# One V block of head 26 on partitions 0 to 63, in two loads of 32 rows

## The chip, the cores and the metric

The kernel runs on one core of a Trainium2 chip. The metric is the device time of one execution in microseconds; less is better. All data is 32-bit floating point.

## The reference, cut to what matters

One token passes through attention and a small MLP, twice, with the same weights and the same caches both times. There are 32 heads, 8192 cached positions and 128 numbers to a head, so each pass reads 128 MB of K and 128 MB of V (the second pass keeps a little of the first's data).

```python
def _A_ref(x, k_cache, v_cache, wq, wo):
    q = (x @ wq).reshape(B, Sq, H, Dh) ...
    scores = jnp.einsum("bhqd,bhkd->bhqk", q, k_cache) * (Dh ** -0.5)
    p = _softmax(scores, axis=-1)
    o = jnp.einsum("bhqk,bhkd->bhqd", p, v_cache)
    return ... o.reshape(B, Sq, H * Dh) @ wo
def _B_ref(x, w1, w2):
    return relu(x @ w1) @ w2

x = x + _A_ref(_layernorm(x), k_cache, v_cache, wq, wo)
x = x + _B_ref(_layernorm(x), w1, w2)
x = x + _A_ref(_layernorm(x), k_cache, v_cache, wq, wo)
x = x + _B_ref(_layernorm(x), w1, w2)
```

## The kernel before, in words

K and V are streamed from device memory through a ring in on-chip memory, `ring`, 128 partitions by 4808 units of 8 numbers. The host lays the caches out beforehand (`_laid_out`), so that each load is one contiguous piece of `kv`, and every partition gets one contiguous row of it. Row sizes in the listings below are in numbers: a load `128x8192` is 128 rows of 8192 numbers, 4 MB.

A head's K is four pieces and its V four blocks; each of the eight is 1 MB. `UNITS` says which pieces share a load. From head 4 to 23 heads are joined, in loads of 6 or 5 MB; heads 24 to 27 have one 4 MB load for K and one for V; heads 0, 1 and 28 to 31 have smaller loads. `ORDER` lists the units, `HEADS` the order of the heads in each pass: 0 to 31 in the first, 31 down to 24 and then the others in the second. Some units of heads 29 to 31 are kept from the first pass to the second.

What sets the order of the loads is `pump`. It takes the next unit of the list `todo`, asks `place` for room in the ring, issues the load on SP's queue, and goes on until no room is left. `release`, called after the last product that reads a piece, frees its room and calls `pump` again. SP issues in that order and waits, for each load, until the products that read the old data are done, and until an earlier load has landed whose completion semaphore the new load takes over. A few loads of weights are issued by ScalarE (ACT's queue).

For each head TensorE multiplies the K pieces with the query (`scores`), VectorE takes the maximum, ScalarE the exponentials, and `turn` transposes them, one block of 128 columns at a time, in squares of 32 by 32, into `hd.all_p`. `values` then multiplies each V block: four products, one for each strip `g` of 32 output rows, of all 128 partitions with 4 columns of the turned exponentials. A V block lies over all 128 partitions: 128 rows of 2048 numbers. `output` adds up the strips, and the next head begins. After the last head of a pass come the output projection and the MLP, whose loads of weights (`part_of_w2`, `mix`) and whose reuse of the ring join the two passes.

The lines that the prediction's steps touch: the ring loads are L189 in `pump`, the products of `scores` L516, those of `values` L570, the transpositions L552 in `turn`.

Of the kernel before, what the change touches and what calls it, by code (L numbers as in the profile page):

```python
# [10 lines left out]
F32 = mybir.dt.float32  # L11
# [4 lines left out]
P = 128  # L16
D = 640
H = 32
SK = 8192
DH = 128  # L20
# [15 lines left out]
K_ALL = [(r, 0, RUN) for r in range(4)]  # L36
V_ALL = [(b, 0, 4) for b in range(NBL)]
# [3 lines left out]
UNITS = {h: WHOLE for h in range(H)}  # L41
# [12 lines left out]
    ("v", V_ALL[2:]),  # L54
]
UNITS[30] = HALVES
UNITS[28] = [("k", K_ALL[:1]), ("k", K_ALL[1:2])] + HALVES[1:]
UNITS[31] = HALVES[:2] + LAST
PAIR = [
# [10 lines left out]
UNITS = {  # L70
    h: [[(h, kind, piece) for piece in pieces] for kind, pieces in units]
    for h, units in UNITS.items()
}
# [8 lines left out]
ORDER = [(h, i) for h in range(H) for i in range(len(UNITS[h]))]  # L82
# [14 lines left out]

def wide(kind, piece):

    return 4 * piece[2] * (1 if kind == "k" else DH) // 8  # L100


def size(u):
    return sum(wide(kind, piece) for _, kind, piece in UNITS[u[0]][u[1]])
# [17 lines left out]
def w2_width(blocks):  # L122
    return sum(D // 2 if b == FB - 1 else D for b in blocks)
# [3 lines left out]
def decode_kernel(ctx: ExitStack, tc: tile.TileContext, x, kv, wq, wo, wqo, w1, w2, out):  # L127
    nc = tc.nc
    consts = ctx.enter_context(tc.tile_pool(name="consts", bufs=1))
    wts = ctx.enter_context(tc.tile_pool(name="wts", bufs=1))  # L130
    work = ctx.enter_context(tc.tile_pool(name="work", bufs=1))
# [9 lines left out]
    ring = consts.tile([P, 8 * (RING + W2_UNITS)], F32, name="ring")  # L141
# [6 lines left out]

    beside = todo[n_first : n_first + BESIDE]
    del todo[n_first : n_first + BESIDE]  # L150
    dram_at, o = {}, 0
    for u in ORDER:
        dram_at[u] = o
        o += 8 * P * size(u)
    live = {}
    lent = set()
    at_of = {}
# [2 lines left out]
    def place(layer, u, n):  # L160


        step = 8 if u in KEPT else max(m for m in (8, 64, 256, 512) if n % m == 0)
        low, high = 0, FLAT if u[0] >= 28 else 3 * BIG
        if layer and (u[0] >= 28 or u[0] < HG):
            high = RING
        if n > FLAT // 3:
            step, high = BIG, 3 * BIG
        if layer == 0 and u in kept and (u in KEPT or u[0] == 30 and UNITS[30][u[1]][0][1] == "k"):
            low, high = (EDGE, RING) if u in KEPT else (FLAT, EDGE)  # L170
        at, best = low, None
        for a, m in sorted(live.values()) + [(high, 0)]:
            a = min(a, high)
            if a - at >= n and (best is None or a - at < best[1]):
                best = at, a - at
            at = max(at, -(-(a + m) // step) * step)
        return None if best is None else best[0]

    def pump():
        while todo:  # L180
            layer, u = todo[0]
            n = size(u)
            at = place(layer, u, n)
            if at is None:
                return
            todo.pop(0)
            o = dram_at[u]
            stays = PARK_ROW if (layer, u) == (1, PARKED) else 0
            nc.sync.dma_start(  # L189
                ring[:, 8 * at + stays : 8 * (at + n)],  # L190
                kv[o : o + 8 * P * n].rearrange("(p m) -> p m", p=P)[:, stays:],
            )
            if stays:
                for a, bank in parked:
                    nc.scalar.copy(ring[:, 8 * at + a : 8 * at + a + bank.shape[1]], bank)
            for t, (_, kind, piece) in enumerate(UNITS[u[0]][u[1]]):
                m = wide(kind, piece)
                live[layer, u, t] = at, m
                at_of[layer, u, t] = ring, 8 * at
                at += m  # L200
            if not todo or layer < todo[0][0]:
                assert all(a + m <= RING for a, m in live.values())
                live["w2"] = RING, W2_UNITS
                for part in W2_LOADS[layer][:2]:
                    part_of_w2(layer, part, by_parts[:, part[0] * D :])
                if layer == 0:
                    part_of_w2(0, W2_LOADS[0][2], wct.rearrange("p c d -> p (c d)"))
        rest = W2_LOADS[1][2:]
        if (1, rest[0][0]) not in w2_block:
            n = w2_width(sum(rest, ()))  # L210
            at = place(1, (0, None), n // 8)
            if at is not None:
                at *= 8
                for part in rest:
                    part_of_w2(1, part, ring[:, at:])
                    at += w2_width(part)

    def part_of_w2(L, blocks, where):
        loads = W2_LOADS[L]
        o = P * w2_width(sum(loads[: loads.index(blocks)], ()))  # L220
        n = w2_width(blocks)
        nc.sync.dma_start(where[:, :n], w2[L, o : o + P * n].rearrange("(p m) -> p m", p=P))
        at = 0
        for b in blocks:
            m = w2_width((b,))
            w2_block[L, b] = where[:, at : at + m]
            at += m
# [17 lines left out]
    def key(L, u, t):  # L245
        return (0 if u in kept else L), u, t
# [45 lines left out]
    load_wq(0, nc.sync)  # L292
    nc.scalar.dma_start(xr, x)
    pump()
    load_wo(0, 0, nc.sync)

# [251 lines left out]

    def turn(hd):

        for b in range(NBL):
            nc.vector.transpose(hd.all_p[:, b * P : (b + 1) * P], hd.p[:, b * P : (b + 1) * P])  # L552

# [6 lines left out]
        nc.vector.reciprocal(hd.rl, pt[:, :1])  # L560

    def values(hd, piece, where, first, last):
        b, r, m = piece
        tile_of, at = at_of[key(*where)]
        ranges = ((r, r + m),) if hd.out is hd.out_2 else ((r, min(r + m, 2)), (max(r, 2), r + m))
        for r0, r1 in ranges:
            for g in range(4) if r0 < r1 else ():
                i = 4 * b + g
                v = at + (g * m + r0 - r) * DH
                nc.tensor.matmul(  # L570
                    (hd.out if r0 < 2 else hd.out_2)[
                        32 * g : 32 * g + 4, r0:r1
                    ].rearrange("p r d -> p (r d)"),
                    hd.all_p[:, 32 * i : 32 * i + 4],
                    tile_of[:, v : v + (r1 - r0) * DH],
                    start=first,
                    stop=last or (hd.out is not hd.out_2 and b == NBL - 1),
                    skip_group_check=True,
                )
        release(*where)  # L580
# [485 lines left out]
def _laid_out(A_x, A_k_cache, A_v_cache, A_wq, A_wo, B_w1, B_w2):  # L1066
    k = np.asarray(A_k_cache)[0].reshape(H, 4, 4, RUN, DH).transpose(0, 4, 1, 2, 3)
    v = np.asarray(A_v_cache)[0].reshape(H, 4, 4, NBL, 4, 32, DH).transpose(0, 1, 5, 3, 4, 2, 6)
    v = v.reshape(H, P, NBL, 4, 4, DH)
    kv = np.empty(H * P * SK * 2, k.dtype)  # L1070
    o = 0
    for u in ORDER:
        n = 8 * size(u)
        block = kv[o : o + P * n].reshape(P, n)
        o += P * n
        a = 0
        for h, kind, piece in UNITS[u[0]][u[1]]:
            if kind == "k":
                r, c, m = piece
                part = k[h, :, :, r, c : c + m]  # L1080
            else:
                b, r, m = piece
                part = v[h, :, b, :, r : r + m]
            part = part.reshape(P, -1)
            block[:, a : a + part.shape[1]] = part
            a += part.shape[1]
    w2 = np.zeros((P, FB, D), np.asarray(B_w2).dtype)
    for b, f in enumerate(_hidden_rows()):
        w2[f >= 0, b] = np.asarray(B_w2)[f[f >= 0]][:, _COLS]
    w2[W2_LAST:, -1, : D // 2] = w2[:W2_LAST, -1, D // 2 :]  # L1090
    wq = np.asarray(A_wq).reshape(NB, P, NG, HG * DH).transpose(2, 1, 0, 3).reshape(NG, P, HG * D)
    wo = np.asarray(A_wo)[:, _COLS].reshape(NG, HG, DH, D).transpose(0, 2, 1, 3)
    wqo = [
        [np.concatenate([wq[b], wo[a].reshape(P, HG * D)], 1) for a, b in zip(gs[1:-1], gs[2:])]
        for gs in GROUPS
    ]
    return {
        "x": np.repeat(np.asarray(A_x).reshape(D)[_COLS].reshape(4, DR), 32, axis=0),
        "kv": kv,
        "wq": wq.reshape(NG * P, HG * D),  # L1100
        "wo": wo,
        "wqo": np.array(wqo),
        "w1": np.asarray(B_w1).reshape(NB, P, DFF).transpose(1, 0, 2),
        "w2": np.array(
            [
                np.concatenate(
                    [
                        np.concatenate([w2[:, b, : w2_width((b,))] for b in part], 1).reshape(-1)
                        for part in loads
                    ]  # L1110
                )
                for loads in W2_LOADS
            ]
        ),
    }
# [24 lines left out]
```

## Time and profile before

| what | value |
|---|---|
| median of three runs | 1344.15 us (1343.68 to 1344.17) |
| span of the profiled execution, first to last instruction | 1340.6 us |
| TensorE (PE) busy | 874.0 us, 65% |
| VectorE (DVE) busy | 290.2 us, 22% |
| ScalarE (ACT) busy | 62.6 us, 5% |
| moved by DMA | 571.70 MB, 426 GB/s on average |
| mean granted TensorE clock | 0.820 |

The profiled execution is one of its own; its own time is known by its span, 1340.6 us, and the runs' times hold what lies around a span too. A page of the profile has the busy time of each engine, the span in 40 slices, the DMA queues, the chain of work that ended last (followed back from the last instruction to whatever released it), the costliest groups of instructions, and the DMA issues with their size and the time from issue to landing. Other views give the same for a stretch of time. PE is TensorE's products, PEld its weight loads, SP the engine that only issues loads. A product of 32-bit numbers stands as two records on PE. "<-" behind an idle time names what ended it.

### The profile page before, as it was taken

What the parts mean: (1) busy time and instruction counts of PE and PEld (TensorE: products, weight loads), DVE (VectorE), ACT (ScalarE), POOL (GpSimd) and SP (SyncE); (2) the same over time, 40 slices, a digit from 0 to 9 for tenths busy, and PEclk for the clock granted to TensorE, in tenths of its full rate; (3) what the DMA queues carried; (4) which work ended last, traced back from release to release, by engine and by line L of the source; (5) the groups of instructions that cost most, each with busy time, mean ns of one, the idle gap of its engine ahead of it and who ended that gap; (6) DMA issues with size and microseconds to landing.
All of it is one profiled execution on the core that took longest, in us unless ns stands there. A gap on an engine that the chain in (4) does not pass through costs nothing.

```text
span 1340.6 us, 13403 instructions
## 1 busy us (share of the span) xinstructions
PE 874.0 (65%) x5806; PEld 255.5 (19%) x5806; DVE 290.2 (22%) x956; ACT 62.6 (5%) x155; POOL 2.9 (0%) x10
## 2 busy tenths in 40 slices
PE   5463575767657656676688755657566666567687
PEld 2110121111111111112243211112111111111123
DVE  2120121211212112223123212221221212212222
ACT  0000000000000000000000000000000000000000
POOL 0000000000000000000000000000000000000000
PEclk8686787988777887788799977887778787888789
DMA  9999999999999999999999999999999999999998
GB/s 395 431 435 430 442 423 437 429 428 437 432 434 429 428 439 426 433 425 415 425 396 425 430 435 433 432 433 431 433 429 434 432 428 433 437 427 436 425 424 333
DMA packets 24546, 571.70 MB, mean 426 GB/s; under 512 B 2724, under 2 KB 2984, under 8 KB 6952
## 3 DMA queue, kind: packets, MB, share of 16 engines
q1 hardware_dynamic: 21464, 529.31, 92.1%
q10 hardware_dynamic: 3024, 41.53, 7.3%
q8 instruction: 46, 0.75, 0.2%
q14 instruction: 12, 0.10, 0.0%
HBM read 570.83 MB, written 0.00 MB: 426 GB/s over the span
## 4 chain that ended last, share of the span: by engine, by line
DMA 67%; PE 27%; DVE 4%; ACT 1%; issue 1%; SPq 0%; ACTq 0%; DVEq 0%
DMA ring<-in_kv 66%; PE ps L516 10%; PE outs L570 9%; PE side L672 1%; DMA ring<-in_w 1%; DVE p L591 1%; PE acc L621 1%; PE side L440 1%; ACT p L545 1%; DVE h_t L531 1%; PE small L536 1%; PE small L604 1%; PE side L454 1%; DVE p L552 0%; DVE h_t L537 0%
## 5 line engine op out<-in xcount | busy, mean ns | idle before, releaser
L516 PE MATMUL ps<-ring,spread_q 128*32 128x512 f32 (+3 forms) x2088 | 332.7, 727 | 149.2 <-DMA ring<-in_kv 148.6
L570 PE MATMUL outs<-ring,p 128*4 128x512 f32 (+3 forms) x2080 | 310.6, 732 | 164.1 <-DMA ring<-in_kv 95.7
L531 DVE TENSOR_REDUCE h_t<-ps 128x1 f32<-128x512 f32 x64 | 44.3, 691 | 365.4 <-PE ps L516 365.4
L570 PEld LDWEIGHTS outs<-ring,p 128*4 128x4 f32 x2080 | 50.6, 95 | 348.4 <-issue 233.8
L516 PEld LDWEIGHTS ps<-ring,spread_q 128*32 128x32 f32 x2088 | 63.9, 124 | 277.5 <-issue 188.8
L545 ACT ACTIVATE p<-ps,h_t 128x512 f32<-128x512 f32 x63 | 43.3, 687 | 1161.2 <-DVE h_t L537 1161.2
L552 DVE STREAM_TRANSPOSE p<-p 128x128 f32<-128x128 f32 x256 | 79.8, 312 | 63.9 <-ACT p L545 57.2
L587 DVE TENSOR_SCALAR p<-outs,ind 128x128 f32<-128x128 f32 x64 | 22.5, 351 | 317.2 <-PE outs L570 317.2
L604 PE MATMUL small<-ones,p 128*128 128x1 f32 (+1 forms) x128 | 25.3, 267 | 97.4 <-DVE p L591 97.4
L591 DVE SCALAR_TENSOR_TENSOR p<-outs,ind,p 128x128 f32<-128x128 f32 x188 | 66.0, 351 | 6.7
L536 PE MATMUL small<-ident,h_t 128*128 128x128 f32 x128 | 32.7, 339 | 40.1 <-DVE h_t L531 39.9
L604 PEld LDWEIGHTS small<-ones,p 128*128 128x128 f32 x128 | 19.9, 195 | 159.7 <-DVE p L591 158.9
L672 PE MATMUL side<-w_t,wct 128*128 128x448 f32 (+1 forms) x80 | 45.3, 651 | 0.0
L452 DVE TENSOR_SCALAR q_row<-side,ln_r 128x128 f32<-128x128 f32 x56 | 19.5, 349 | 106.0 <-PE ps L516 59.0
L440 PE MATMUL side<-both_t,ln_xc 128*32 128x512 f32 x140 | 37.3, 844 | 0.0
L536 PEld LDWEIGHTS small<-ident,h_t 128*128 128x128 f32 x128 | 20.0, 196 | 89.0 <-DVE h_t L531 85.5
L621 PE MATMUL acc<-both_t,o_cols 128*64 128x320 f32 x220 | 34.6, 458 | 0.0
L454 PEld LDWEIGHTS side<-sel,q_row 128*128 128x128 f32 x112 | 19.3, 216 | 56.3 <-DVE q_row L452 29.9
L537 DVE TENSOR_REDUCE h_t<-small 128x1 f32<-128x128 f32 x64 | 18.7, 292 | 35.4 <-PE small L536 35.4
L454 PE MATMUL side<-sel,q_row 128*128 128x1 f32 x112 | 24.1, 284 | 0.3 <-DVE q_row L452 0.2
L621 PEld LDWEIGHTS acc<-both_t,o_cols 128*64 128x64 f32 x220 | 15.5, 147 | 29.4 <-issue 17.7
L672 PEld LDWEIGHTS side<-w_t,wct 128*128 128x128 f32 x80 | 13.5, 211 | 32.4 <-issue 32.4
(148 smaller groups left out, 219.5 us busy)
## 6 DMA issues: line engine op xcount, KB each, us to landing
ring<-in_kv SPq DMA_DIRECT2D x50, 6144.0 KB, 35.0
ring<-in_kv SPq DMA_DIRECT2D x23, 4096.0 KB, 33.2
ring<-in_kv SPq DMA_DIRECT2D x29, 2048.0 KB, 27.7
both_t<-in_wqo ACTq DMA_DIRECT2D x12, 2560.0 KB, 24.7
ring<-in_kv SPq DMA_DIRECT2D x4, 5120.0 KB, 34.6
ring<-in_kv SPq DMA_DIRECT2D x9, 1024.0 KB, 23.9
w_t<-in_w ACTq DMA_DIRECT2D x1, 4320.0 KB
ring<-in_kv SPq DMA_DIRECT2D x5, 768.0 KB, 29.5
```

The costliest lines, as they stand in the source:

```text
L440: nc.tensor.matmul(pq[32 * strip : 32 * strip + 32], xc[:, c : c + 1].to_broadcast([P, 32]), wq_t[:, c], start=c < 4, stop=c in (1, 2, 3, ...
L454: nc.tensor.matmul(mine[:, :1], row, one_of_each, start=True, stop=True, skip_group_check=True)
L516: nc.tensor.matmul(hd.ps[32 * g : 32 * g + 32, c : c + n], spread_q[:, 3 - r : 35 - r], tile_of[:, at + g * n : at + (g + 1) * n], start=f ...
L531: nc.vector.tensor_reduce(hd.nm, hd.ps, AX.X, ALU.max, negate=True)
L536: nc.tensor.matmul(pt[:, :P], hd.nm.to_broadcast([P, P]), ident, start=True, stop=True)
L545: nc.scalar.activation(hd.p, hd.ps, AF.Exp, bias=hd.low, scale=scale, accum_out=hd.l)
L552: nc.vector.transpose(hd.all_p[:, b * P : (b + 1) * P], hd.p[:, b * P : (b + 1) * P])
L570: nc.tensor.matmul((hd.out if r0 < 2 else hd.out_2)[32 * g : 32 * g + 4, r0:r1].rearrange("p r d -> p (r d)"), hd.all_p[:, 32 * i : 32 * i ...
L591: nc.vector.scalar_tensor_tensor(oc, hd.out[:, r], ind[:, r : r + 1], oc, op0=ALU.mult, op1=ALU.add)
L604: nc.tensor.matmul(pt[:, :n], part, mask.to_broadcast([P, n]), start=i == 0, stop=i == len(parts) - 1,)
L621: nc.tensor.matmul(acc[64 * g : 64 * g + 64, : 2 * DR], col.to_broadcast([P, 64]), wt[:, 2 * DR * g : 2 * DR * (g + 1)], start=first, stop ...
L672: nc.tensor.matmul(pt[:, :n], wct[:, c], w1_t[:, c, f : f + n], start=(c == 0), stop=(c == NB - 1),)
```

## The change

The first V block of head 26 (block 0, 1 MB) gets a unit of its own, `LOW_BLOCK`, and is laid on partitions 0 to 63 only, with rows twice as long: 64 rows of 4096 numbers. Row r holds what partitions r and r + 64 held. In device memory it stands as two times eight groups; a group is four rows, one behind another, and 64 unused numbers follow it, so that neighbouring groups don't run on into each other. `pump` loads it with two loads of 32 rows, each from eight groups. The other three blocks of that V stay one load of 3 MB.

In `turn`, the exponentials of the upper 64 partitions are transposed a second time, into partitions 0 to 63 of a small tile (`by_act`), and `values` multiplies the block in eight products of 64 partitions, four with the lower half and four with that tile. In the ring the block takes twice its former columns (512 units in place of 256): `place` puts it at columns 4096 to 4607 of the units in both passes, above the rest, and the places of some loads after it move. Head 26 is loaded in both passes, so all this happens twice.

```diff
+LOW_BLOCK = (0, 0, 4, "low")
+UNITS[26] = [("k", K_ALL), ("v", [LOW_BLOCK]), ("v", V_ALL[1:])]
...
-    return 4 * piece[2] * (1 if kind == "k" else DH) // 8
+    return 4 * piece[2] * (1 if kind == "k" else DH) // 8 * (1 + is_low(piece))
+def is_low(piece):
+    return len(piece) > 3
+LOW_ENGINES = 8
+LOW_GAP = 64
+def low_group(n):
+    return 32 // LOW_ENGINES * 8 * n + LOW_GAP
...
+            if low_unit(u):
+                m = LOW_ENGINES * low_group(n)
+                for half in range(2):
+                    nc.sync.dma_start(
+                        ring[32 * half : 32 * half + 32, 8 * at : 8 * (at + n)],
+                        kv[o + half * m : o + half * m + m]
+                        .rearrange("(g m) -> g m", g=LOW_ENGINES)[:, : low_group(n) - LOW_GAP]
+                        .rearrange("g (r m) -> g r m", m=8 * n),
+                    )
+            else:
...
     def turn(hd):
+        low = [piece for piece, _ in pieces_of(0, hd.h, "v") if is_low(piece)]
+        for b, *_ in low:
+            hd.upper = work.tile([P, 2, DH], F32, name="by_act")[:64, 0]
+            nc.vector.transpose(hd.upper, hd.p[64:, b * P : (b + 1) * P])
         for b in range(NBL):
             nc.vector.transpose(hd.all_p[:, b * P : (b + 1) * P], hd.p[:, b * P : (b + 1) * P])
...
     def values(hd, piece, where, first, last):
+        if is_low(piece):
+            for half, turned in enumerate((hd.all_p[:64, b * P : (b + 1) * P], hd.upper)):
+                for g in range(4):
+                    v = at + (4 * half + g) * 4 * DH
+                    nc.tensor.matmul(
+                        hd.out[32 * g : 32 * g + 4].rearrange("p r d -> p (r d)"),
+                        turned[:, 32 * g : 32 * g + 4],
+                        tile_of[:64, v : v + 4 * DH],
+                        start=first and half == 0,
+                        stop=last and half == 1,
+                        skip_group_check=True,
+                    )
+            release(*where)
+            return
```

On SP's queue, in the first pass, around heads 24 to 28 (`128x8192` rows are K or V of a whole head), there stands before:

```order
L189 DMA ring<-in_kv 128x12288 x17
L189 DMA ring<-in_kv 128x8192 x8
L189 DMA ring<-in_kv 128x2048 x2
L189 DMA ring<-in_kv 128x4096 x3
L189 DMA ring<-in_kv 128x704
```

and now:

```order
L223 DMA ring<-in_kv 128x12288 x17
L223 DMA ring<-in_kv 128x8192 x5
L216 DMA ring<-in_kv 32x1x4096 x2
L223 DMA ring<-in_kv 128x6144
L223 DMA ring<-in_kv 128x8192 x2
L223 DMA ring<-in_kv 128x2048 x2
```

The load of V of head 26, the sixth of the eight, has become three: two of 32 rows of 4096 numbers and one of 128 rows of 6144. The order of the others is the same; the second pass has the same three in place of one.

On TensorE, at head 26 in the first pass (the rows `side` and `both_t` are the queries of the next group of heads, `small<-ident` the maximum of all rows), before:

```order
L516 MATMUL ps<-ring,spread_q 32x512 x4
L454 MATMUL side<-sel,q_row 128x1
L536 MATMUL small<-ident,h_t 128x128
L570 MATMUL outs<-ring,p 4x512 x4
L454 MATMUL side<-sel,q_row 128x1
L570 MATMUL outs<-ring,p 4x512 x12
L604 MATMUL small<-ones,p 128x1
```

and now:

```order
L550 MATMUL ps<-ring,spread_q 32x512 x4
L488 MATMUL side<-sel,q_row 128x1
L570 MATMUL small<-ident,h_t 128x128
L607 MATMUL outs<-ring,p 4x512 x4
L607 MATMUL outs<-ring,by_act 4x512 x4
L488 MATMUL side<-sel,q_row 128x1
L622 MATMUL outs<-ring,p 4x512 x12
L656 MATMUL small<-ones,p 128x1
```

The first block's four products have become eight, four of them with the second transposition; the other twelve follow as before. On VectorE one transposition of 64 by 128 stands ahead of the head's four.

More of the change, by code (lines that the diff above doesn't have):

```diff
@@ L98, in wide, with low_unit, placed_in_dram @@
 def wide(kind, piece):
-    return 4 * piece[2] * (1 if kind == "k" else DH) // 8
+    return 4 * piece[2] * (1 if kind == "k" else DH) // 8 * (1 + is_low(piece))
+def is_low(piece):
+    return len(piece) > 3
+def low_unit(u):
+    return any(is_low(piece) for _, _, piece in UNITS[u[0]][u[1]])
+LOW_ENGINES = 8
+LOW_GAP = 64
+def low_group(n):
+    return 32 // LOW_ENGINES * 8 * n + LOW_GAP
+def placed_in_dram():
+    at, o = {}, 0
+    for u in ORDER:
+        at[u] = o
+        o += 2 * LOW_ENGINES * low_group(size(u)) if low_unit(u) else 8 * P * size(u)
+    return at, o
 def size(u):
@@ L150, in decode_kernel @@
     del todo[n_first : n_first + BESIDE]
[L151 to L154, printed above, removed]
+    dram_at, _ = placed_in_dram()
     live = {}
@@ L188, in pump @@
             stays = PARK_ROW if (layer, u) == (1, PARKED) else 0
[L189 to L192, printed above, removed]
+            if low_unit(u):
[8 more added lines that the diff above has]
+            else:
+                nc.sync.dma_start(
+                    ring[:, 8 * at + stays : 8 * (at + n)],
+                    kv[o : o + 8 * P * n].rearrange("(p m) -> p m", p=P)[:, stays:],
+                )
             if stays:
@@ L562, in values @@
     def values(hd, piece, where, first, last):
-        b, r, m = piece
+        b, r, m = piece[:3]
         tile_of, at = at_of[key(*where)]
+        if is_low(piece):
[9 more added lines that the diff above has]
+                        skip_group_check=True,
+                    )
+            release(*where)
+            return
         ranges = ((r, r + m),) if hd.out is hd.out_2 else ((r, min(r + m, 2)), (max(r, 2), r + m))
@@ L1069, in _laid_out @@
     v = v.reshape(H, P, NBL, 4, 4, DH)
-    kv = np.empty(H * P * SK * 2, k.dtype)
-    o = 0
+    dram_at, total = placed_in_dram()
+    kv = np.zeros(total, k.dtype)
     for u in ORDER:
-        n = 8 * size(u)
+        n, o = 8 * size(u), dram_at[u]
+        if low_unit(u):
+            ((h, _, (b, *_)),) = UNITS[u[0]][u[1]]
+            block = v[h, :, b].reshape(2, 2, 32, n // 2).transpose(1, 2, 0, 3)
+            m = LOW_ENGINES * low_group(size(u))
+            kv[o : o + 2 * m].reshape(2 * LOW_ENGINES, -1)[:, :-LOW_GAP] = block.reshape(
+                2 * LOW_ENGINES, -1
+            )
+            continue
         block = kv[o : o + P * n].reshape(P, n)
-        o += P * n
         a = 0
```

## The prediction

> **What bounds the kernel now.** I read the page of the profile first: its head, the slices, the queues and the chain of waits.
>
> ```profile
> span 1340.6 us, 13403 instructions
> PE 874.0 (65%) x5806; PEld 255.5 (19%) x5806; DVE 290.2 (22%) x956; ACT 62.6 (5%) x155; POOL 2.9 (0%) x10
> ...
> DMA  9999999999999999999999999999999999999998
> ...
> DMA packets 24546, 571.70 MB, mean 426 GB/s; under 512 B 2724, under 2 KB 2984, under 8 KB 6952
> ...
> q1 hardware_dynamic: 21464, 529.31, 92.1%
> q10 hardware_dynamic: 3024, 41.53, 7.3%
> q8 instruction: 46, 0.75, 0.2%
> ...
> DMA 67%; PE 27%; DVE 4%; ACT 1%; issue 1%; SPq 0%; ACTq 0%; DVEq 0%
> ```
>
> The 16 DMA engines are at work in every slice. The loads of the two hardware queues fill 92.1% + 7.3% = 99.4% of 16 engines' span, while TensorE is busy for 65% of it. So the kernel is a stream of 571.70 MB, and the only room left is in how evenly the 16 engines share it. I therefore looked at short stretches: in the middle of each pass, where the V of head 26 is loaded, and at the two ends of the stream. The columns are the stretch, its length, the busy time of PE, PEld, DVE, ACT and POOL, the granted clock, the busy share of the 16 DMA engines, and GB/s.
>
> ```profile
> 570.00:580.00 10.00, 6.16 (x42) 1.49 (x35) 1.56 (x5) 0.00 (x0) 0.00 (x0) 0.84 1.00 429
> 785.00:795.00 10.00, 5.33 (x34) 1.19 (x34) 2.15 (x8) 0.00 (x0) 0.00 (x0) 0.83 1.00 429
> ...
> 1331.00:1332.00 1.00, 0.74 (x21) 0.63 (x25) 0.17 (x1) 0.00 (x0) 0.00 (x0) 1.00 0.83 334
> 1332.00:1333.00 1.00, 1.00 (x36) 0.96 (x32) 0.00 (x0) 0.00 (x0) 0.00 (x0) 1.00 0.58 242
> 1333.00:1334.00 1.00, 1.00 (x30) 0.71 (x20) 0.08 (x2) 0.00 (x0) 0.00 (x0) 1.00 0.59 242
> 1334.00:1335.00 1.00, 0.99 (x26) 0.76 (x25) 0.87 (x6) 0.00 (x0) 0.00 (x0) 1.00 0.49 197
> 1335.00:1336.00 1.00, 0.81 (x19) 0.59 (x15) 0.23 (x3) 0.00 (x0) 0.15 (x1) 1.00 0.37 133
> 1336.00:1337.00 1.00, 0.96 (x28) 0.39 (x20) 0.00 (x0) 0.00 (x0) 0.40 (x1) 1.00 0.02 8
> ```
>
> In the middle the share is 1.00 and all 16 together move 429 GB/s, so one engine moves 429/16 = 26.8 GB/s. At the end the share falls in steps. From 1332 to 1334 it is 0.58 to 0.59, which is 9 of 16 engines; from 1334 to 1335 it is 0.49 (8), from 1335 to 1336 0.37 (6), and at 1336.4 or so all are done. So seven engines finish the last loads by about 1332.3 and nine need until 1334.3 to 1336.4. The same picture stands at the end of the first pass, just before the load of `mix` is issued (at 692.67 in the chain below) and reaches the idle engines:
>
> ```profile
> 691.50:692.00 0.50, 0.35 (x4) 0.16 (x8) 0.10 (x1) 0.00 (x0) 0.00 (x0) 1.00 1.02 415
> 692.00:692.50 0.50, 0.50 (x12) 0.24 (x8) 0.00 (x0) 0.00 (x0) 0.00 (x0) 1.00 0.71 292
> 692.50:693.00 0.50, 0.50 (x14) 0.25 (x5) 0.32 (x1) 0.00 (x0) 0.00 (x0) 1.00 0.66 248
> 693.00:693.50 0.50, 0.50 (x5) 0.44 (x4) 0.34 (x3) 0.31 (x2) 0.00 (x0) 1.00 0.44 179
> 695.00:695.50 0.50, 0.50 (x24) 0.48 (x20) 0.00 (x0) 0.00 (x0) 0.00 (x0) 1.00 1.06 435
> ```
>
> Some engines are out of work from 692 on (0.71, then 0.66 of 16), only seven still run at 693.25 (0.44), and by 695 all work on what came next. The engines thus drift apart by 3 to 4 us in each pass, although every load gives each of them the same bytes. The 46 packets of the instruction queue are the one thing on the page that can fall on some engines and not on others; the page doesn't say on which. The chain of waits says what the late ones cost:
>
> ```profile
> 573.46 34.55 DMA ring<-in_kv
> 608.14 5.36 PE outs L570 x32
> ...
> 692.67 4.72 DMA mix<-in_w
> 697.43 0.75 PE side L482 x16
> ...
> 1286.31 30.14 DMA ring<-in_kv
> 1316.50 19.15 DMA ring<-in_w
> ```
>
> A load counts as landed when its last engine has delivered. The chain runs through such landings, and its last link ends at 1316.50 + 19.15 = 1335.65, among the nine late engines. The latest engine sets the time; one that is done early saves nothing.
>
> **The change part by part.** *The bytes.* The block is 64 rows of 4096 numbers, 1,048,576 bytes, as before. Before, all 16 engines carry it, 65,536 bytes each, inside the 4 MB load. Now two loads of 32 rows come from eight contiguous groups. No row of this trace shows how such a load is shared out, so its price lies between two bounds: if all 16 engines share it, nothing moves (0); if each group is one engine's, eight engines carry 131,072 bytes each and the other eight none. Then eight gain 65,536 / 26.8 GB/s = 2.45 us of work in each pass and eight lose as much. I take the second, since eight sources of one piece each are nearest to the rows of one engine in the loads there are; both ends stay in the range.
>
> The Trainium skill, "DMA: Bandwidth & Descriptors", under "Why a DMA increments its semaphore by 16 and not by 1", says that a load runs on the largest number of engines up to 16 that divides the slowest dimension of both sides, and on the lowest-numbered ones; 8 and 32 would give eight engines, the same eight twice. No run so far shows it. The same page's "Rules for kernel authors" says of transfers to partition halves that both spray over all 16 engines, so that nothing is won; by that rule the sum would be 0 instead of 2.45 us a pass, which is the first rival below.
>
> *What 2.45 us do at the end of a pass.* Only seven engines have that much slack at the end (those done by 1332.3). Eight get the extra work, so at least one late engine is among them. At best it is the first of the nine, and 1334.3 + 2.45 = 1336.75, or 0.35 us after today's 1336.4; at worst it is the last, +2.45. Six engines end between 1335 and 1336.4. If lateness has nothing to do with the half that is loaded, three of those six are loaded, the last of the three ends about 0.3 us before the last of the six, and the pass gets 2.45 - 0.3 = 2.15 us longer. At the end of the first pass nine engines are idle at 693.25, so the bounds there are 0 and +2.45; the same reasoning gives 2.15. I take 2.15 twice: the rows show no order by halves, and with half of the engines loaded at random the six latest are spared almost never.
>
> *Why it isn't absorbed in between.* Where the stream is full the share is 1.00: the late engines have no idle time that could take the extra work. Between the passes the loads that follow the `mix` load are issued after work that itself waited for the last landing, so a later landing shifts them too.
>
> *Issues on SP.* Each pass has two more loads, three issues instead of one. The rows that show SP's lead are these (size, then median us from issue to landing; then whom SP waits for):
>
> ```profile
> ring<-in_kv SPq DMA_DIRECT2D x23, 4096.0 KB, 33.2
> ring<-in_kv SPq DMA_DIRECT2D x9, 1024.0 KB, 23.9
> ...
> SPq L189 <- DMA ring<-in_kv: 367.3, 77, 20.6
> ```
>
> A 4 MB load takes 4,194,304 / 429 = 9.8 us on the engines and lands 33.2 us after its issue, so SP runs more than 20 us ahead. What hides two more issues, or a load that waits for a later landing, is this lead: 0. If it were gone, a wait of SP on a ring load is 367.3/77 = 4.8 us, once or twice a pass. The block's place at the top of the ring moves the places of the loads around it, and with them what a load waits for: in the first pass the last part of head 28 now waits for two K pieces of head 27 instead of the last V piece of head 26, and in the second pass K of head 27 waits for a V piece of head 29. Both are within the lead.
>
> *TensorE and VectorE.* The block needs eight products of 64 rows in place of four of 128, and one more transposition:
>
> ```profile
> 588.68 1.84 PE L570 MATMUL outs<-ring,p 128*4 128x512 f32 x8 [1.87 <-DMA ring<-in_kv]
> 787.44 4.95 PE L570 MATMUL outs<-ring,p 128*4 128x512 f32 x32 [4.41 <-DMA ring<-in_kv]
> L552 DVE STREAM_TRANSPOSE p<-p 128x128 f32<-128x128 f32 x256 | 79.8, 312 | 63.9 <-ACT p L545 57.2
> ```
>
> These are the first products of head 26's V in the two passes (eight records are four products). They take up to 1.84 us a block, so four more cost up to 1.84 us a pass, and the transposition at most 312 ns, as for a whole block. TensorE waited 1.87 and 4.41 us for the V there. The low block is issued ahead of the other three blocks, so its products fall into that wait: 0. If the cover were gone, the ring would be freed about 2 us later, still within SP's lead.
>
> **Sum:** 2 x 2.15 = +4.3 us on the profiled execution's 1340.6 us span. The median of the runs, 1344.15, lies 3.55 us above that span, which I take to be what lies around it, unchanged: 1344.15 + 4.3 = 1348.4 us.
>
> **The rivals.** *Nothing moves.* The two loads are spread over all 16 engines, as by the rule named above, or the end isn't as tight as the tail says. For it: no row shows a load on eight engines. Against it: the source lies in eight separate pieces. It gives 1344.2 us, with the small costs above within 0.5 us.
>
> *The slack is on the loaded side.* If the seven early engines are all among the eight loaded, the extra falls where there is room. It gives 0.35 us at the end and 0 to 2 us after the first pass, so +0.4 to +2.7: 1346 us. For it: lateness comes in a group (seven against nine), and a group may well follow the engines' numbers. Against it: nothing on the page ties it to a half, and nine don't fit into eight.
>
> *The other side: faster.* The late engines all lie in the lightened half and the loaded half takes its extra inside its slack. Then each pass ends 2.45 us earlier, 2 x 2.45 = 4.9 us: 1339.3 us. It decides from the point where at least eight engines are done 2.45 us before the last. At 692.5 to 693.5 that could be so (9 of 16 idle at the end of it); at 1333 to 1334 the share of 0.59 says nine still run, one too many. Elsewhere the runs without a profile may differ from this one.
>
> **How the numbers follow.** A change of 0.2%, 2.7 us, is about what a measurement of this kernel can tell from none. Extra work on late engines (+3.5 to +4.9, 1347.6 to 1349.1): 0.60. Slack on the loaded side (+0.4 to +2.7, 1344.5 to 1346.9): 0.20. Nothing moves: 0.13. Faster: 0.07. I predict the first, 1348.4. The range must leave out no more than 0.2: it reaches from 1344.3, which takes in the second case and half of the third, to 1349.6, the bound of 2 x 2.45 with the small costs on top. Slower by over 0.2% has the first case and a third of the second: 0.66; within 0.2% the rest of the second and the third: 0.27; faster 0.07.
>
> **What would show it.** If the two loads run on eight engines, the DMA share in the stretch after they start stays at 1.00 but the ends of the passes change: the steps of the tail come at other heights, with some engines done 2.45 us sooner and the last one 2 us later. The chain should keep its links, with the last landing of each pass later by 2.15 us. A new wait of SP or TensorE near 590 or 790 us would show my cover wrong. A tail in which all 16 engines end within a microsecond would be the faster rival; an unchanged tail the first. The prediction is wrong if a load of 32 rows uses all 16 engines, or if lateness follows the halves.

## The result, and the profile after

The changed kernel takes 1348.06 us (median of five, 1346.8 to 1352.15). The kernel before, run beside it, takes 1344.03 (1343.33 to 1344.17). The ratio is 1.0035, with a 95% interval of 1.0023 to 1.0047: 3.1 to 6.3 us slower. The prediction was 1348.4.

The page of the profiled execution, in the order in which that of before was shown:

```profile
span 1345.0 us, 13440 instructions
PE 897.7 (67%) x5822; PEld 259.7 (19%) x5822; DVE 290.9 (22%) x958; ACT 62.5 (5%) x155; POOL 2.9 (0%) x10
...
DMA packets 24706, 571.70 MB, mean 425 GB/s; under 512 B 2756, under 2 KB 3016, under 8 KB 6984
...
q1 hardware_dynamic: 21624, 529.31, 91.9%
...
q8 instruction: 46, 0.75, 0.2%
```

The bytes are the same, and the stream still fills the span (91.9% of 16 engines in q1). The packets say on how many engines the new loads ran. q1 has 160 more than before, and 32 more are under 512 B. e5 below, whose two added loads are plain ones of 128 rows, has 288 packets more than before, 32 of them small: 128 + 16 for each load. So a load shows one data packet for each row and, it seems, one small packet for each engine that carries it. The two passes have four new loads of 32 rows: 4 x 32 = 128 data packets more (the old block's rows were part of longer ones, and that load still has its 128), and 4 x 8 = 32 small ones. By this count each load ran on eight engines. The Trainium skill, "DMA: Bandwidth & Descriptors", under "Why a DMA increments its semaphore by 16 and not by 1", gives eight for sides of 8 and 32; the 32 small packets agree. The other rule that the prediction named, by which both parts would spray over all 16, doesn't hold for these loads.

The stretches of time, columns as in the prediction (busy PE, PEld, DVE, ACT, POOL; granted clock; busy share of 16 DMA engines; GB/s). First the two in the middle of the passes:

```profile
570.00:580.00 10.00, 5.93 (x42) 1.58 (x35) 1.56 (x5) 0.00 (x0) 0.00 (x0) 0.84 0.99 423
785.00:795.00 10.00, 7.22 (x42) 1.27 (x38) 2.59 (x8) 0.78 (x2) 0.00 (x0) 0.67 1.02 440
```

The new loads lie there, and the stream runs on at its old rate. Then the end of the kernel:

```profile
1335.00:1336.00 1.00, 1.00 (x8) 0.94 (x8) 0.62 (x4) 0.37 (x2) 0.00 (x0) 1.00 0.78 315
1336.00:1337.00 1.00, 0.74 (x22) 0.63 (x25) 0.17 (x1) 0.00 (x0) 0.00 (x0) 1.00 0.73 284
1337.00:1338.00 1.00, 1.00 (x36) 0.96 (x32) 0.00 (x0) 0.00 (x0) 0.00 (x0) 1.00 0.33 131
1338.00:1339.00 1.00, 1.00 (x30) 0.71 (x22) 0.07 (x1) 0.00 (x0) 0.00 (x0) 1.00 0.18 74
1339.00:1340.00 1.00, 1.00 (x26) 0.77 (x25) 0.87 (x6) 0.00 (x0) 0.00 (x0) 1.00 0.27 92
1340.00:1341.00 1.00, 0.99 (x22) 0.77 (x22) 0.24 (x3) 0.00 (x0) 0.14 (x1) 1.00 0.07 24
```

and the end of the first pass:

```profile
693.00:693.50 0.50, 0.21 (x2) 0.07 (x1) 0.22 (x1) 0.00 (x0) 0.00 (x0) 1.00 0.35 143
693.50:694.00 0.50, 0.48 (x8) 0.25 (x12) 0.00 (x0) 0.00 (x0) 0.00 (x0) 1.00 0.24 97
694.00:694.50 0.50, 0.50 (x16) 0.20 (x8) 0.00 (x0) 0.00 (x0) 0.00 (x0) 1.00 0.15 61
694.50:695.00 0.50, 0.50 (x10) 0.30 (x2) 0.45 (x2) 0.00 (x0) 0.00 (x0) 1.00 0.22 92
```

Before, nine of 16 engines were late together (0.58, 0.59). Now most are done by about 1337, and some three (0.18) to four (0.27) work alone until after 1340. The first pass ends the same way: 0.15 to 0.24 from 693.5 on. This is what extra work on a few engines that were late already would look like; the trace doesn't say which engines they are. The chain of waits has the first pass's delay in two links:

```profile
650.93 35.21 DMA ring<-in_kv
694.54 5.21 DMA mix<-in_w
```

The first ends at 686.14 (before 648.54 + 35.72 = 684.26), 1.88 us later; `mix` lands at 699.75 (before 697.39), 2.36 us later.

At the end of the kernel the chain doesn't keep its links. Before, its last link was a load, to 1335.65. Now it has no load behind the one that these products wait for (in the kernel before, the same products began at 1289.15 and waited for no load):

```profile
1291.72 1.89 PE L622 MATMUL outs<-ring,p 128*4 128x512 f32 x8 [4.53 <-DMA ring<-in_kv]
```

From 1310 on TensorE waits for a load only once:

```profile
PEld side L987 <- DMA ring<-in_w: 0.3, 1, 0.3
```

So in this execution the lonely engines and TensorE arrive together, and the tail alone doesn't set the end.

How late the stream is can be counted from the packets of the traces: the time at which the two hardware queues have moved a number of MB, less the time before (us; one profiled execution each; e5 and e10 are explained below).

| moved | 270 MB | 310 MB | 320 MB | 570 MB | 570.8 MB |
|---|---|---|---|---|---|
| time before | 630.2 | 727.8 | 751.6 | 1332.1 | 1335.6 |
| changed kernel | +0.1 | +2.4 | +3.2 | +3.3 | +4.2 |
| e5: even shares in both passes | +0.2 | +1.0 | +3.0 | +3.1 | +3.5 |
| e10: eight engines in the first pass only | +0.2 | +1.9 | +2.3 | +2.6 | +2.7 |

Nothing is lost while the block is loaded (270 MB lie behind the first pass's block), nor between 320 and 570 MB. The changed kernel loses 2.3 us up to 310 MB, around the end of the first pass, 0.8 us behind it, where e5 loses more, and 0.9 us in the last 0.8 MB.

### The profile page after: what moved, and what is told of

The parts are those of the page before. It is cut to its first block, busy times and chain, and to the rows that moved or that the text cites. A ratio compares the mean times of both kernels' runs of the same rounds, so it can differ in the third digit from the quotient of the medians.

```text
span 1345.0 us, 13440 instructions
## 1 busy us (share of the span) xinstructions
PE 897.7 (67%) x5822; PEld 259.7 (19%) x5822; DVE 290.9 (22%) x958; ACT 62.5 (5%) x155; POOL 2.9 (0%) x10
## 3 DMA queue, kind: packets, MB, share of 16 engines
q1 hardware_dynamic: 21624, 529.31, 91.9%
## 4 chain that ended last, share of the span: by engine, by line
DMA 60%; PE 32%; DVE 5%; ACT 1%; issue 1%; SPq 0%; ACTq 0%; DVEq 0%
DMA ring<-in_kv 60%; PE ps L550 11%; PE outs L622 11%; PE side L724 2%; PE side L474 2%; DVE p L643 2%; ACT p L579 1%; DVE h_t L565 1%; PE acc L673 1%; PE small L570 1%; PE side L488 1%; PE small L656 1%; DVE p L590 1%; DVE h_t L571 1%; DVE p L639 1%
## 5 line engine op out<-in xcount | busy, mean ns | idle before, releaser
L622 PE MATMUL outs<-ring,p 128*4 128x512 f32 (+3 forms) x2064 | 327.4, 772 | 163.4 <-DMA ring<-in_kv 92.5
## 6 DMA issues: line engine op xcount, KB each, us to landing
ring<-in_kv SPq DMA_DIRECT2D x21, 4096.0 KB, 33.3
ring<-in_kv SPq DMA_DIRECT2D x4, 5120.0 KB, 33.2
```

Of the source, the lines that this page charges most:

```text
L622: nc.tensor.matmul((hd.out if r0 < 2 else hd.out_2)[32 * g : 32 * g + 4, r0:r1].rearrange("p r d -> p (r d)"), hd.all_p[:, 32 * i : 32 * i ...
```

## The experiments

The run times of each round of experiments stand beside runs of the kernel before on the same chip, with medians of 1343.4 to 1343.6 us; the changed kernel's stand beside 1344.03. The chip isn't the same in every round, so runs are compared by their ratios. The code below is shortened; `...` stands for what is left out.

| kernel | median us | ratio to before, 95% interval |
|---|---|---|
| changed kernel | 1348.06 | 1.0035 (1.0023 to 1.0047) |
| e5: block on all 128 rows | 1344.95 | 1.0009 (1.0001 to 1.0018) |
| e10: low block in the first pass only | 1346.67 | 1.0024 (1.0014 to 1.0034) |
| e1: sixteen groups of two rows | 1354.91 | 1.0087 (1.0073 to 1.0101) |
| e2: eight in pass one, sixteen in pass two | 1351.95 | 1.0057 (1.0045 to 1.0070) |
| e3: K piece from eight groups | 1360.39 | 1.0124 (1.0110 to 1.0138) |
| e4: K piece from four groups | 1378.60 | 1.0261 (1.0246 to 1.0277) |
| e6: K piece from sixteen groups | 1353.50 | 1.0070 (1.0058 to 1.0082) |
| e7: one load of 64 rows, sixteen groups | 1354.03 | 1.0078 (1.0065 to 1.0091) |
| e8: four groups of eight rows | 1375.49 | 1.0237 (1.0222 to 1.0253) |
| e9: one load of 64 rows, eight groups | 1361.90 | 1.0132 (1.0119 to 1.0146) |
| e11: more code | 1348.08 | 1.0036 (1.0023 to 1.0049) |
| e12: same time, little code | 1353.01 | 1.0070 (1.0058 to 1.0082) |

### First controls, and a miss: the same block or another load, shared out differently

e1 was meant to undo the imbalance and nothing else.

```diff
-LOW_ENGINES = 8
+LOW_ENGINES = 16
```

> The changed kernel with one number changed: the two 32-row loads come from sixteen groups of two rows in place of eight of four. Ring places, issues, products and the second transposition stay as changed. Balance theory (the two loads burden eight engines with 2.45 us a pass): with sixteen groups all engines share the load and all of the 4.0 us goes, 1344.0 to 1344.6 us. Rival (the extra products and transposition, the extra issues, or the moved places in the ring cost it): those are all still there, 1347.5 to 1348.5.

It got worse, 1354.91 us: neither theory. The stretches show why:

```profile
575.00:580.00 5.00, 0.38 (x2) 0.30 (x2) 0.98 (x4) 0.00 (x0) 0.00 (x0) 0.65 0.89 210
580.00:585.00 5.00, 3.53 (x20) 1.00 (x24) 0.00 (x0) 0.00 (x0) 0.00 (x0) 0.50 0.97 226
585.00:590.00 5.00, 5.00 (x34) 1.34 (x26) 1.05 (x3) 0.00 (x0) 0.00 (x0) 0.82 1.04 442
```

All engines are busy (0.89 to 0.97), but they move 210 to 226 GB/s in place of 429, for some ten us. The share of busy time alone doesn't show it; the GB/s beside it does. Counted as above, the stream of e1 loses 5.1 us between 240 and 250 MB and 5.3 us between 330 and 335 MB, where the block is loaded: nearly all of the 12.3 us by which it reaches 570.8 MB later than before.

e2 loads the block from eight groups in the first pass and from sixteen in the second.

```diff
-LOW_ENGINES = 8
+LOW_ENGINES = (8, 16)
...
+                e = LOW_ENGINES[layer]
```

> The changed kernel with the block stored twice: the first pass loads it from eight groups, the second from sixteen. Balance theory with both ends tight, as predicted: half of the loss, 2.15 us, 1346.0 to 1346.4. Rival one (only the last landing of the kernel counts, the drift of the first pass is made up between the passes): 1344.0 to 1344.6. Rival two (the whole cost arises in the first pass): 1348.

It gives 1.0057, near the mean of the changed kernel and e1, 1.0061. The passes add up, but with the half rate in the second it doesn't tell whether both ends are tight.

e3 and e4 put the same imbalance on another load of the kernel before, a K piece of head 28 on 128 rows.

```diff
+GROUPED = (28, 0)
+GROUPS_OF = (8, 8)
...
+                nc.sync.dma_start(
+                    ring[:, 8 * at : 8 * at + a],
+                    kv[o : o + m].rearrange("(g m) -> g m", g=g)[:, : P // g * a]
+                    .rearrange("g (r m) -> g r m", m=a),
+                )
```

> The kernel before, with nothing but the source of one other 1 MB load changed in both passes (the first K piece of head 28): its 128 rows stand in eight groups of 16 rows with 64 unused numbers behind each. It still lands on all 128 partitions at its old place; no product, no transposition, no issue and no place is new. Balance theory: eight engines carry 131,072 bytes of it in place of 65,536, the same +2.45 us, and the whole 4.0 to 4.4 us comes back: 1348.0 to 1348.6. If the number of groups doesn't decide (rather the 32 partitions of the destination), or if products and places cost it: 1344.0 to 1344.6.

> As the kernel before with that K piece of head 28 in eight groups, but four groups of 32 rows. Balance theory: four engines carry 262,144 bytes in place of 65,536, 196,608 / 26.8 GB/s = +7.34 us a pass, twelve lose 2.45. If the four are among the seven early ones (done by 1332.3 where the last is done at 1336.4), a pass ends at 1332.3 + 7.34 = 1339.6, 3.2 us later: +6.5, 1350.6. If one of the four is the latest: +14.7, 1358.8; one in the middle of the late nine gives 1356 or so. If the load is spread over sixteen all the same: 1344.2.

In e4 `GROUPS_OF` is (4, 4). Both miss by far: 1360.39 and 1378.60. They too have stretches at half rate; e3's first:

```profile
605.00:610.00 5.00, 0.06 (x1) 0.00 (x0) 1.59 (x6) 0.78 (x2) 0.00 (x0) 0.84 0.94 215
610.00:615.00 5.00, 2.31 (x12) 0.45 (x16) 0.00 (x0) 0.00 (x0) 0.00 (x0) 0.50 1.00 228
```

and e4's:

```profile
610.00:615.00 5.00, 4.75 (x24) 0.91 (x28) 0.00 (x0) 0.00 (x0) 0.00 (x0) 0.50 1.05 224
615.00:620.00 5.00, 1.82 (x14) 0.45 (x6) 1.56 (x5) 0.00 (x0) 0.00 (x0) 0.84 1.02 224
```

In e4 four groups carry the load, and yet all sixteen engines together are busy at half speed: engines that carry other loads are held up too. The packets of this trace say it directly: those of 16,384 bytes, which the regrouped load with its rows of 8,192 doesn't have, took 1120 to 1435 ns from 610 to 620; in the changed kernel, from 575 to 580, such packets took 611 to 621 ns. So there is a cost that the changed kernel itself doesn't have (429, then 423 GB/s). These runs can't test the balance; they ask what it is about the changed kernel's loads that spares it.

### The balance by itself

e5 brings the block in one plain load of 128 rows. The split of the V, the room in the ring, the second transposition and eight products stay. Besides the engines' shares it thus changes three things: one load in place of two, a source without gaps, and all partitions in place of 64.

```diff
-                for half in range(2):
-                    nc.sync.dma_start(ring[32 * half : 32 * half + 32, ...], ... eight groups ...)
+                nc.sync.dma_start(
+                    ring[:, 8 * at : 8 * at + 4 * n],
+                    kv[o : o + 4 * P * n].rearrange("(p m) -> p m", p=P),
+                )
...
+            for rows in (64, 128):
+                ... four products of hd.all_p[:rows], start=True ...
```

> The changed kernel, but the block lies on all 128 partitions and comes in one plain load of 128 rows. Its room in the ring (512 units), the split of the V into 1 MB and 3 MB, the second transposition and eight products stay (four of 64 rows, which the four of 128 rows then overwrite). Balance theory: every engine carries 65,536 bytes again, so all of the 4.0 us goes: 1343.3 to 1344.5. Rival (products, transposition, split or places cost it): 1347.5 to 1348.5.

Most of the loss goes: 1344.95, ratio 1.0009 (0.1 to 2.4 us). The last engines are again many together:

```profile
1335.00:1336.00 1.00, 1.00 (x36) 0.96 (x32) 0.00 (x0) 0.00 (x0) 0.00 (x0) 1.00 0.61 251
1336.00:1337.00 1.00, 1.00 (x36) 0.72 (x26) 0.00 (x0) 0.00 (x0) 0.00 (x0) 1.00 0.56 230
1337.00:1338.00 1.00, 0.95 (x26) 0.84 (x28) 0.69 (x4) 0.00 (x0) 0.00 (x0) 1.00 0.52 206
1338.00:1339.00 1.00, 0.82 (x18) 0.47 (x10) 0.48 (x3) 0.00 (x0) 0.00 (x0) 1.00 0.30 102
```

Nine of 16 (0.56) down to eight (0.52), as in the kernel before; the three that work alone for some 3 us are gone. So the way in which the block is loaded is what costs. That it is the shares, and not the additional load or the gaps, is argued from the traces: nothing is lost where the block is loaded, and SP's lead is the same (a 4 MB load lands 33.3 us after its issue, before 33.2). By the ratios the loading is worth 1.0035 - 1.0009 = 0.26%, 3.5 us, give or take 2; the remaining 1.2 us are more than the expectation's 1344.5 allowed and just outside no change.

e10 has the eight engines in the first pass and e5's plain load in the second.

```diff
-            if low_unit(u):
+            if low_unit(u) and layer:
+                ... one plain load of 128 rows, from a second copy of the block ...
+            elif low_unit(u):
```

> The changed kernel in the first pass; in the second the block comes in one plain load of 128 rows, with room in the ring, split, products and transposition as changed. So eight engines carry it in the first pass alone, without the doubled rate loss of the run with sixteen groups. Balance theory with both ends tight, as predicted: half of what the engines' shares cost, 1.2 to 2 us, on top of what the run on 128 rows kept (about 1 us): 1345.7 to 1347.0. If only the last landing counts: 1344.3 to 1345.3. If the whole cost arises in the first pass: 1347.5 to 1348.5.

1346.67, ratio 1.0024, within the first theory's 1345.7 to 1347.0 and between e5 and the changed kernel: this fits a part for each pass, by the ratios 0.15% (2.0 us, give or take 1.8) for the first and 0.11% (1.5 us, give or take 2.1) for the second. The second is not clear of nothing, and e10's own interval, 1345.3 to 1348.0, touches both rivals. Its profiled execution was the fastest of its eight (1344.72). The end of the kernel there, where the second pass is plain, has nine together again:

```profile
1334.00:1335.00 1.00, 1.00 (x40) 0.96 (x32) 0.00 (x0) 0.00 (x0) 0.00 (x0) 1.00 0.73 297
1335.00:1336.00 1.00, 1.00 (x32) 0.72 (x28) 0.00 (x0) 0.00 (x0) 0.00 (x0) 1.00 0.54 223
1336.00:1337.00 1.00, 1.00 (x28) 0.88 (x30) 0.65 (x4) 0.00 (x0) 0.00 (x0) 1.00 0.58 236
```

### What halves the stream

Three more runs asked whether it is the gaps in the source, the number of engines on a part of the partitions, or who writes where. e6 is e3 with sixteen groups of 8 rows:

```diff
-GROUPS_OF = (8, 8)
+GROUPS_OF = (16, 16)
```

> The kernel before with the first K piece of head 28 in sixteen groups of 8 rows in device memory, 64 unused numbers behind each, landing on 128 partitions as before. By rows, an engine should carry what it carries in a plain load; only the gaps in the source are new. If the gaps halve the stream (the 215 to 230 GB/s that stood for 15 us in the run with eight groups): 1355 to 1360 again. If it is which engine writes which partitions: 1343.3 to 1344.4, and no stretch near 214 GB/s.

e7 reads the changed kernel's very groups, in one load in place of two:

```diff
-                for half in range(2):
-                    nc.sync.dma_start(ring[32 * half : 32 * half + 32, ...], ... g=LOW_ENGINES ...)
+                nc.sync.dma_start(ring[:64, ...], ... g=2 * LOW_ENGINES ...)
```

> The changed kernel with the block's two loads in one: 64 rows from the same sixteen groups of four rows, so sixteen engines write partitions 0 to 63. If a half of the partitions takes no more than the eight engines that fill it in plain loads (8 x 26.8 = 214 GB/s), the stream halves as it did with sixteen groups for 32 rows: 1353 to 1356. If 32 partitions take 214 GB/s each, there is neither contention nor imbalance: 1343.5 to 1344.5.

e8 has four groups of eight rows to each 32-row load (`LOW_ENGINES = 4`).

> The changed kernel with four groups of eight rows for each 32-row load: four engines carry the whole block, 262,144 bytes each, +7.34 us a pass, and twelve carry none, -2.45. Balance theory: if the four are all early ones (done 4.1 us ahead of the last), a pass gets 7.34 - 4.1 = 3.2 us longer, 1350.6; if a late one is among them 5 to 7.3 us a pass, 1354 to 1358.8. If the cost of the change were the products or the places: 1348 as for eight groups. A stretch at half the rate would show contention besides.

All three fall to half rate. The rows of e7, e6 and e8, in this order:

```profile
580.00:585.00 5.00, 3.09 (x16) 0.87 (x17) 0.00 (x0) 0.00 (x0) 0.00 (x0) 0.50 0.90 213
...
605.00:610.00 5.00, 0.13 (x2) 0.00 (x0) 1.59 (x6) 0.78 (x2) 0.00 (x0) 0.85 0.92 220
...
580.00:585.00 5.00, 5.00 (x32) 1.20 (x24) 0.70 (x2) 0.00 (x0) 0.00 (x0) 0.69 0.96 215
```

e7 acquits the source: it reads the changed kernel's bytes from the same gapped groups, and costs 10.5 us where that costs 4.7 (by the ratios). It fits a limit of 214 GB/s on partitions 0 to 63, but e6 doesn't: there sixteen engines write all 128. And e8's four engines stay below any such limit; e8's 1375.49 tells nothing on four engines' balance, for the same reason as e4. What fits all is a smaller unit, a port. Say that partitions 4g to 4g+3 and 32+4g to 35+4g (g from 0 to 7), and the same above 64, share one way in that takes what one engine brings, and that a plain load keeps one engine to each. The changed kernel's group g is exactly rows 4g to 4g+3 in the first load and 32+4g to 35+4g in the second: each way has one engine. In e7 engines g and g+8 meet on each; in e6 rows 0 and 32 begin the groups of engines 0 and 4. e9 was made to decide: the shares of the changed kernel, eight engines on partitions 0 to 63, only the rows grouped by eights.

```diff
-    return 32 // LOW_ENGINES * 8 * n + LOW_GAP
+    return 64 // LOW_ENGINES * 8 * n + LOW_GAP
...
-                for half in range(2):
+                nc.sync.dma_start(ring[:64, ...], ... g=LOW_ENGINES ...)
```

> The changed kernel with the block's two loads in one of 64 rows, from eight groups of eight rows (not two times eight groups of four). The same number of engines carries the same bytes each; only which rows go together changes: group 0 writes partitions 0 to 7 and group 4 partitions 32 to 39. Port theory: partitions 4g to 4g+3 and 32+4g to 35+4g share one way in that takes what one engine brings (26.8 GB/s), and plain loads keep one engine to each; here two engines meet on each of them, and the stream halves as in the runs with sixteen groups: 1353 to 1360. Capacity theory (a half of the partitions takes 214 GB/s, whoever writes): eight engines fit, 1347.5 to 1348.5 as in the changed kernel. The Trainium skill, 'SBUF - State Buffer', under 'Door 1: The DMA port swizzle', has these eight partitions on one of 16 ports; by it the port theory holds.

1361.90, the port theory's side and above its range; the limit by halves is out. The stream falls to half rate again, for about five us, and stays below the full one for five more (313 GB/s):

```profile
575.00:580.00 5.00, 0.38 (x2) 0.30 (x2) 0.51 (x2) 0.00 (x0) 0.00 (x0) 0.90 0.88 221
```

The Trainium skill, "SBUF — State Buffer", under "Door 1: The DMA port swizzle", has these eight partitions on one of 16 ports, and partitions 0 to 63 on eight of them. These runs agree: 210 to 228 GB/s wherever, by that reading, two engines meet on a port. Which engine writes which rows stands in no trace, though. Nor does a run put an engine on rows other than those of a plain load without two engines meeting, so "two meet" and "an engine away from its usual rows" aren't told apart. And half rate isn't all of e9's cost: of the 19.2 us by which it reaches 570.8 MB later, 4.3 and 5.4 are lost where the block is loaded, and the rest around and behind the end of the first pass and in the last bytes.

### Why some engines are late

The prediction put the drift down to the instruction queue's packets, as a guess. e11 adds code that moves no data, e12 is its control.

```diff
 def turn(hd):
+        for _ in range(24 if hd.h not in (0, 31) else 0):
+            nc.tensor.matmul(outs_row[:32, :1], ident[:, :32], ones, start=True, stop=True)
```

```diff
 def turn(hd):
+        for _ in range(6 if hd.h not in (0, 31) else 0):
+            nc.tensor.matmul(outs_row, ident, ones.to_broadcast([P, 512]), start=True, stop=True)
```

> The kernel before, with 24 tiny products (128x32 weights, one column) more in each of 60 heads' passes, while TensorE waits for the exponentials. They move no data, but are 24 x 4 instructions a head, half as many again as the kernel has: some 23 more packets in the instruction queue (46 before; 0.2% of 16 engines' span is about 0.9 us a packet). If such packets make the late engines late and fall on eight of them: 23 / 8 x 0.9 = 2.6 us, 1345.5 to 1347.5. If they fall on all sixteen alike: 1.3 us, 1344.7. If they cost nothing: 1343.3 to 1344.2. If TensorE's extra time matters: 1348 or more, and the next run shows it too.

> The control for the run with more code: the kernel before with six products of 512 columns in the same places, at 0.46 us each 2.8 us of TensorE's time a head, but only 24 instructions, some 6 more packets. If the packets cost the time there, this one stays within 0.7 us of the kernel before: 1343.3 to 1344.7. If it is TensorE's time: as long as that run or longer.

The queue took 22 packets more in e11:

```profile
PE 991.7 (74%) x8686; PEld 364.8 (27%) x8686; DVE 290.1 (22%) x956; ACT 62.5 (5%) x155; POOL 2.9 (0%) x10
...
q8 instruction: 68, 1.11, 0.3%
```

and five more in e12, whose chain of waits changed hands:

```profile
PE 1081.7 (80%) x6526; PEld 374.6 (28%) x6526; DVE 290.1 (22%) x956; ACT 62.5 (5%) x155; POOL 2.9 (0%) x10
...
q8 instruction: 51, 0.84, 0.3%
...
PE 48%; DMA 46%; DVE 5%; issue 1%; ACT 0%; SPq 0%; DVEq 0%; ACTq 0%
```

e11 lost 4.7 us, but the control lost 9.6 with TensorE at 80% and 48% of the chain. TensorE had less room than assumed, so e11's loss can't be given to the packets. What makes some engines late stays open.

## Why the prediction was right, point by point

*The stream bounds the kernel; the last engine sets the time.* Held for the stream: same bytes, q1 at 91.9%, the middle at its old rate, and most of the loss around the end of the first pass and in the last bytes. That the last engine alone sets the end held less well: in the profiled execution TensorE, which had waited 4.53 us for an earlier load, arrives together with the last engines. The sign that the prediction named, a chain that keeps its links, is there in the first pass and not at the end of the second.

*The loads run on eight engines, +2.45 us each.* The eight follow from the packets. The 2.45 us fit the tail: three or four engines go on for some 3 us after the others.

*At least one late engine is loaded; 2.15 us a pass, twice.* The first pass agrees: its two links came 1.88 and 2.36 us later. But with even shares (e5) `mix` lands at 698.33, 0.94 us later, so about 1.4 of the 2.36 are the shares'. The second pass brings less in the profiled execution: 0.9 us in the last 0.8 MB, inside the prediction's bounds of 0.35 to 2.45. The 0.8 us between the passes are no matter of the shares, as e5 loses some 2 us there. So 2 x 2.15 met a growth of the span by 4.4 that is made up otherwise, about 2.4 + 0.8 + 0.9 and the rest; that the sum fits so closely is partly luck. By the medians e5 and e10 give 3.5 us, 2.0 and 1.5 a pass: the term was somewhat too large if anything, within the intervals.

*The span and the runs.* The prediction took the 3.55 us between the median and the span as what lies around a span. Every run that lists its span shows 1.7 to 2.0 us there (1346.8 to 1345.0 for the changed kernel), so the profiled execution of before was one of some 1342.4 us, faster than the median. The sum doesn't suffer, because the 3.55 us were left unchanged.

*Products, transposition, issues and places at 0.* e5, which keeps them nearly all, costs 1.2 us (0.1 to 2.4). So 4.3 + 0 came out right with perhaps 3.5 + 1.2 behind it; which of the small costs the 1.2 us are stays open. The granted clock doesn't sort the runs: among those of the kernel before it went from 0.796 to 0.827, and the run at 0.796 took 1343.16 us. The cover named for the products was the wrong one. The timeline of the changed kernel, first products of the block in each half:

```profile
588.73 1.88 PE L607 MATMUL outs<-ring,p 64*4 64x512 f32 x8 [1.92 <-DVE p L590]
590.40 1.93 PE L607 MATMUL outs<-ring,by_act 64*4 64x512 f32 x8
592.77 3.92 PE L622 MATMUL outs<-ring,p 128*4 128x512 f32 x24
599.51 3.64 PE L550 MATMUL ps<-ring,spread_q 128*32 128x512 f32 x32 [0.81 <-DMA ring<-in_kv]
```

TensorE waits there for the transposition, not for V, which has landed; the second half-block's 1.93 us lie open, and then TensorE still waits 0.81 us for the next K (2.06 before; in the second pass 1.82, before 2.75). The cover is that later wait.

*The rivals.* Nothing moves: out, since the kernel is slower by 3.1 to 6.3 us. Slack on the loaded side (up to 2.7): the time speaks against it, and so does a tail in which a few engines end some 3 us after the others; e5's 3.5 us, give or take 2, alone wouldn't exclude it. Faster: out by the time.

*The step that was missing.* The prediction gave "if all 16 engines share it, nothing moves (0)" as a bound. By their sixteen groups e1 and e7 do that and cost 11.7 and 10.5 us by their ratios. The sum took an engine's 26.8 GB/s as its own wherever it writes; in these runs that held only for some groupings, by the port reading only as long as no two engines meet. The change's groups of four rows in loads of 32 then happen to give each engine the port that it has in a plain load. That the changed kernel was spared is luck: with groups of eight rows the same reasoning would have said 1348.4, and 1361.9 is what e9 took.

## What to carry to other kernels

In a stream-bound kernel look at the steps of the DMA share at the ends of the stream: bytes put on an engine that ends late can come out at the end, here about 3.5 of 4.9 us by the medians. Look also at whether the compute engines arrive at the same time. When a load leaves the plain 128-row form, work out who writes which partitions, and read GB/s beside the busy share: engines that are held up count as busy. A control that changes the shares must not change the ports, or it measures something else.

## What the runs showed of the hardware that was not expected

- A load of 1 MB whose groups of rows don't fit the plain layout halved the whole stream, to some 210 to 228 GB/s, also for packets of other loads, for five to ten us and more a pass. It cost 9 to 35 us over the two passes. Two engines that meet on the same eight partitions (4g to 4g+3 and 32+4g to 35+4g) are the reading that fits all of these runs.
- A load from g gapped groups ran on g engines for 4, 8 and 16, if its small packets are one for each engine: under 512 B stand 2700 in e4, 2708 in e3 and 2724 in e6 and before, two loads with 12, 8 and 0 fewer.
